# The first queries of an attention and mixer kernel: loaded by GpSimd with a cast on the way, ahead of the keys, instead of by SyncE's queue

## The chip, the cores and the metric

The kernel runs on one core of a Trainium2 chip. A core has five engines with one instruction stream each: TensorE (PE in the profile, with its weight loads shown apart as PEld), VectorE (DVE), ScalarE (ACT), GpSimd (POOL) and SyncE (SP). Transfers are issued from SyncE's, ScalarE's or GpSimd's stream. The metric is the device time of one execution in microseconds; less is better.

## The reference

Inputs are float32: q, k and v with 8 batches, 12 heads, 448 positions and head size 64, and four weight matrices. For each batch and head, scores are q times k transposed, divided by 8; the attention is the square of the positive part of the scores, divided by 448; it is multiplied with v. The heads side by side make x, of 8 x 448 x 768. A mixer follows:

```
attn = maximum(scale * (q @ k.T), 0) ** 2 / 448
x    = attn @ v, heads joined                      # 8 x 448 x 768
h    = maximum(x.T @ w_tok1, 0) @ w_tok2           # tokens: 448 -> 256 -> 448
u    = x + h.T
out  = u + maximum(u @ w_ch1, 0) @ w_ch2           # channels: 768 -> 1536 -> 768
```

## The kernel before

The 96 heads are worked in 24 groups of four heads ("slots" s; three of them make a batch). The positions of a head are 7 chunks of 64. For each group:

- Loads bring keys, queries and values to SBUF as bfloat16 (`k_raw`, `q_raw`, `v_raw`, four buffers each). The inputs are float32, so the transfer casts, and GpSimd issues it (lines 340 and 350).
- Keys and queries are transposed. For groups 0 to 8 TensorE does it (line 513), with an identity matrix `ident` that GpSimd makes, and ScalarE or VectorE copies the result from PSUM to `kqT` (lines 303 and 305). Later groups use a transposing DMA on SyncE's queue.
- Scores: 7 steps of four 64x64-weight matmuls of 448 columns (line 564, `sc_ps`). ScalarE or VectorE takes the positive part (lines 297 and 299) into `sq`, VectorE squares it in place (line 601).
- Values: 28 matmuls (line 619, `acc_ps`), then an eviction to `xT`, with the scale (lines 649 and 651).
- Token mixing: a transpose of `xT` to `x_sb` (line 704 for the first groups), the product with the first weights (line 741, `t_ps`), its positive part `r_sb`, the product with the second (line 776, `h_ps`), and on VectorE the sum u (line 788, `uT_sb`).

Per batch, channel mixing follows: line 832 (first product, 128-row weights of `wc`) and line 903 (second), whose results VectorE adds to a transposed u and SyncE stores.

The order on the engines is written out before the kernel is built. A class `Planner` holds all operations with their dependencies, an estimated duration and a rank; it steps a clock and gives every engine its next operation. GpSimd's operations alone keep the order in which they were added, that of the string `FIRST` (line 432) at the start. Where two engines can do an operation (`durs`), the planner chooses. Operations of the first batch have an earlier rank (`FRONT`). A transfer is taken to wait for a common ring, with an estimate of its `work`. So a change at the start gives a new order to all engines for the whole run.

Group 0 is special. Its first keys come in two pieces, chunks 0 and 1 (`KCUT` = 2) and chunks 2 to 6. Its queries come as float32 by SyncE's queue (line 320), into the front part of the buffer for output tiles (`out_sb`, not in use yet), and two copies, one on ScalarE and one on VectorE (`wide0`, `wide1`, line 323), cast them into `q_raw`. TensorE first runs 20 matmuls on zeros (`keep_warm`, line 427), then the transposes of all queries of group 0, 3 matmuls on zeros, the transposes of the first key piece, 3 more, the first two score steps, and the transposes of the second key piece. The query transposes wait for all of group 0's queries, the key transposes for their piece alone (line 525):

```
deps = [x for t in ts for x in (loads[s, t] if piece[1:] == (0, KC) else loads[s, t][lo > 0 :][:1])]
```

Of the kernel before, what the change touches and what calls it, by code (L numbers as in the profile page):

```python
# [49 lines left out]
class Planner:  # L50
# [6 lines left out]
    def add(self, op):  # L57
        self.ops.append(op)
        return op
# [160 lines left out]
def kernel(  # L220
# [11 lines left out]
    nc = tc.nc  # L232

    B, H, S, D = q.shape
# [4 lines left out]
    KC = 7  # L239
# [3 lines left out]
    SP = 512  # L243
# [21 lines left out]
    wt1 = sbuf.tile([128, 4, DT], BF16, name="wt1")  # L265
    wt2 = sbuf.tile([128, JC, S], BF16, name="wt2")
    wc1 = sbuf.tile([128, CC, DC], BF16, name="wc1")
    wc2 = sbuf.tile([128, EC, DM], BF16, name="wc2")
    raws = {t: [sbuf.tile([128, 2, KC * D], BF16, name=f"{t}_raw{i}") for i in range(NR)] for t in "kqv"}
# [8 lines left out]
    outs = sbuf.tile([128, NO, DM], FP32, name="out_sb")  # L278
# [5 lines left out]
    add = plan.add  # L284
# [8 lines left out]
    ANY = {"ACT": 0.424, "DVE": 0.534}  # L293
# [7 lines left out]
    def copy(o, out, ps):  # L301
        if o.on == "ACT":
            nc.scalar.activation(out, ps, AF.Copy)
        else:
            nc.vector.tensor_copy(out, ps)  # L305
# [5 lines left out]
    loads = {}  # L311

    def load(s, t):
        src = {"k": k, "q": q, "v": v}[t]
        b, i = divmod(s, GS)
        if t != "v" and s < TDMA:
            from_ = src[b, 4 * i : 4 * i + 4].rearrange("(e h) (p c) d -> (h p) e (c d)", h=2, c=KC)
            if s == 0 and t == "q":
                wide = outs.rearrange("n a m -> n (a m)")[:, : 2 * KC * D].rearrange("n (e m) -> n e m", e=2)
                o = add(Op("ldq0", "SP", lambda o: nc.sync.dma_start(out=wide, in_=from_), dur=0.5, work=1.3, late=-0.5))  # L320
                loads[s, t] = [
                    add(
                        Op(
                            f"wide{e}",
                            ("ACT", "DVE")[e],
                            lambda o, e=e: copy(o, raws[t][0][:, e], wide[:, e]),
                            [o],
                            durs=ANY,
                            slack=0.3,
                            rank=-20,  # L330
                        )
                    )
                    for e in range(2)
                ]
                return
            loads[s, t] = []
            for lo, hi in ((0, KCUT), (KCUT, KC)) if s == 0 else ((0, KC),):

                def emit(o, lo=lo, hi=hi):
                    nc.gpsimd.dma_start(  # L340
                        out=raws[t][s % NR][:, :, lo * D : hi * D], in_=from_[:, :, lo * D : hi * D]
                    )

                loads[s, t].append(add(Op(f"ld{t}{s}.{lo}", "POOL", emit, dur=0.72, work=1.41 * (hi - lo) / KC)))
            return
        for half in range(2):
            h0 = 4 * i + 2 * half

            def emit(o, half=half, h0=h0):
                ins = nc.gpsimd.dma_start(  # L350
                    out=raws[t][s % NR][64 * half : 64 * (half + 1)],
                    in_=src[b, h0 : h0 + 2].rearrange("e (p c) d -> p e (c d)", c=KC),
                )
                if o.gate is not None:
                    tc.add_manual_dep(
                        ins.ins,
                        o.gate.ins.ins.name,
                        mybir.DependencyInfo(mybir.DependencyClass.Sync, mybir.DependencyReason.DATA),
                        reason="load behind crossbar",
                    )  # L360

            o = add(Op(f"ld{t}{s}.{half}", "POOL", emit, dur=0.6, work=0.72))
            loads.setdefault((s, t), []).append(o)
# [65 lines left out]
    for x in xTs:  # L429
        nc.vector.memset(x[:, :, S:], 0.0)  # L430

    FIRST = "k0 q0 id k1 q1 v0 wt1 k2 q2 v1 v2 wt2 k3 q3 wc1 wc1 wc1 v3 k4 q4 v4 k5 q5 v5 wc2 wc2 wc2 k6 q6 v6 k7 q7 v7"
    parts = {"wc1": iter(range(3)), "wc2": iter(range(3))}
    for word in FIRST.split():
        if word == "id":
            id_op = add(Op("ident", "POOL", lambda o: make_identity(nc, ident), dur=0.6))
        elif word == "wt1":
            wt1_ops = load_wt1()
        elif word == "wt2":
            wt2_ops = load_wt2()  # L440
        elif word == "wc1":
            load_wc1(next(parts[word]), 3)
        elif word == "wc2":
            load_wc2(next(parts[word]), 3)
        else:
            load(int(word[1:]), word[0])
    for s in range(8, NS):
        for t in "kqv":
            load(s, t)
# [603 lines left out]
```

## Time and profile before

| | |
|---|---|
| median of four runs | 359.62 us (359.45 to 362.31) |
| the profiled execution | 359.45 us, of it a span of 357.7 us |
| busy PE, DVE, ACT, POOL | 351.1, 231.1, 203.1, 84.4 us |
| first channel-mixing product starts | 32.42 us |
| granted TensorE clock | 1.0 |

The span runs from the first to the last instruction. A line of a timeline has start, duration, engine, line of the kernel, operation, what it writes and reads, how many were merged, and in brackets how long the engine was idle before it and what ended that. "To landing" is the time from a transfer's issue to its semaphore. Shares of the DMA engines are of 16 engines and can pass 100%, since packets overlap.

### The profile page before, as it was taken

What the parts mean: (1) busy time and instruction counts of PE and PEld (TensorE: products, weight loads), DVE (VectorE), ACT (ScalarE), POOL (GpSimd) and SP (SyncE); (2) the same over time, 40 slices, a digit from 0 to 9 for tenths busy, and PEclk for the clock granted to TensorE, in tenths of its full rate; (3) what the DMA queues carried; (4) which work ended last, traced back from release to release, by engine and by line L of the source; (5) the groups of instructions that cost most, each with busy time, mean ns of one, the idle gap of its engine ahead of it and who ended that gap; (6) DMA issues with size and microseconds to landing.
All of it is one profiled execution on the core that took longest, in us unless ns stands there. A gap on an engine that the chain in (4) does not pass through costs nothing.

```text
span 357.7 us, 8785 instructions
## 1 busy us (share of the span) xinstructions
PE 351.1 (98%) x3506; PEld 195.2 (55%) x3506; DVE 231.1 (65%) x428; ACT 203.1 (57%) x421; POOL 84.4 (24%) x141
## 2 busy tenths in 40 slices
PE   8899999999999999999999999999999999999995
PEld 5655545554555555555555555555555555555564
DVE  4998487788697967697767877776856731111032
ACT  5998695678664767843776545752677313412400
POOL 8732522561233303330330330310000000000000
PEclk9999999999999999999999999999999999999999
DMA  8999999999998999999997999976411434113024
GB/s 133 192 212 188 173 207 174 181 219 172 200 179 142 232 183 171 153 191 167 184 116 137 154 198 202 120 124 154 105 31 22 105 81 112 29 47 88 0 66 111
DMA packets 98122, 50.62 MB, mean 142 GB/s; under 512 B 72801, under 2 KB 93857, under 8 KB 98081
## 3 DMA queue, kind: packets, MB, share of 16 engines
q1 hardware_dynamic: 74320, 28.49, 44.3%
q0 software_dynamic: 23600, 21.47, 42.3%
q8 instruction: 27, 0.44, 0.5%
q14 instruction: 15, 0.11, 0.2%
q10 hardware_dynamic: 160, 0.10, 0.1%
HBM read 43.38 MB, written 11.01 MB: 152 GB/s over the span
## 4 chain that ended last, share of the span: by engine, by line
PE 94%; DVE 3%; issue 1%; ACT 1%; ACTq 0%
PE m_ps L832 31%; PE m_ps L903 31%; PE sc_ps L564 10%; PE acc_ps L619 9%; PE t_ps L741 6%; PE h_ps L776 5%; DVE sq L601 2%; PE warm_ps L420 1%; PE kqT_ps L513 1%; PE x_ps L704 1%; DVE kqT L305 0%; ACT sq L297 0%; DVE x_sb L305 0%; DVE uT_sb L788 0%; DVE xT L651 0%
## 5 line engine op out<-in xcount | busy, mean ns | idle before, releaser
L297 ACT ACTIVATE sq<-sc_ps 128x448 bf16<-128x448 f32 x257 | 120.1, 567 | 47.4 <-PE sc_ps L564 47.4
L832 PE MATMUL m_ps<-uT_sb,wc 128*128 128x448 bf16 x576 | 116.0, 353 | 0.0
L903 PE MATMUL m_ps<-wc,r_sb 128*128 128x384 bf16 (+2 forms) x684 | 114.7, 323 | 0.0
L601 DVE TENSOR_TENSOR sq<-sq 128x896 bf16<-128x896 bf16 x168 | 97.6, 619 | 4.5 <-ACT sq L297 3.4
L297 ACT ACTIVATE r_sb<-m_ps 128x448 bf16<-128x448 f32 x96 | 52.7, 551 | 67.5 <-PE m_ps L832 67.3
L903 PEld LDWEIGHTS <-r_sb 128*128 128x128 bf16 x684 | 65.7, 98 | 44.0 <-issue 2.7
L832 PEld LDWEIGHTS <-wc 128*128 128x128 bf16 x576 | 54.9, 98 | 53.5 <-issue 5.9
L937 DVE TENSOR_TENSOR out_sb<-m_ps,u_sb 128x384 f32<-128x384 f32 (+2 forms) x57 | 31.3, 550 | 65.2 <-PE m_ps L903 65.1
L299 DVE TENSOR_SCALAR sq<-sc_ps 128x448 bf16<-128x448 f32 x79 | 47.3, 620 | 23.0 <-PE sc_ps L564 22.9
L350 POOL DMA_DIRECT2D v_raw<-in_v_dram x48 | 28.7, 605 | 128.8 <-PE sc_ps L564 111.2
L564 PE MATMUL sc_ps<-kqT 64*64 64x448 bf16 x672 | 47.5, 356 | 0.9 <-ACT sq L297 0.4
L619 PE MATMUL acc_ps<-sq,v_raw 64*64 64x448 bf16 x672 | 37.2, 350 | 0.2
L788 DVE TENSOR_TENSOR uT_sb<-h_ps,xT 128x448 bf16<-128x448 f32 x48 | 27.7, 617 | 13.7 <-PE h_ps L776 13.7
L564 PEld LDWEIGHTS <-kqT 64*64 64x64 bf16 x672 | 17.0, 105 | 22.0 <-issue 13.0
L619 PEld LDWEIGHTS <-v_raw 64*64 64x64 bf16 x672 | 19.9, 107 | 13.9 <-issue 3.1
L741 PE MATMUL t_ps<-x_sb,wt 128*128 128x256 bf16 (+1 forms) x216 | 25.1, 261 | 0.0
L776 PE MATMUL h_ps<-wt,r_sb 128*128 128x448 bf16 x96 | 22.3, 353 | 0.1
L741 PEld LDWEIGHTS <-wt 128*128 128x128 bf16 x216 | 17.9, 98 | 8.1 <-issue 5.3
L651 DVE TENSOR_SCALAR xT<-acc_ps 128x448 bf16<-128x448 f32 x24 | 14.9, 622 | 8.7 <-PE acc_ps L619 8.7
L350 POOL DMA_DIRECT2D k_raw<-in_k_dram x30 | 18.2, 620 | 6.7 <-DMA kqT<-kqi 5.1
L649 ACT ACTIVATE xT<-acc_ps 128x448 bf16<-128x448 f32 x24 | 13.3, 554 | 10.2 <-PE acc_ps L619 9.5
L350 POOL DMA_DIRECT2D q_raw<-in_q_dram x30 | 18.4, 637 | 1.7 <-issue 1.6
(38 smaller groups left out, 119.0 us busy)
## 6 DMA issues: line engine op xcount, KB each, us to landing
out_dram<-out_sb SPq DMA_DIRECT2D x54, 192.0 KB, 2.9
v_raw<-in_v_dram POOLq DMA_DIRECT2D x48, 112.0 KB, 5.6
wc<-in_moe_w_ch_dram POOLq DMA_DIRECT2D x6, 768.0 KB, 14.1
k_raw<-in_k_dram POOLq DMA_DIRECT2D x30, 112.0 KB, 5.7
q_raw<-in_q_dram POOLq DMA_DIRECT2D x30, 112.0 KB, 6.3
k_raw<-in_k_dram POOLq DMA_DIRECT2D x8, 224.0 KB, 9.1
q_raw<-in_q_dram POOLq DMA_DIRECT2D x8, 224.0 KB, 8.6
u_sb<-uT_sb SPq DMA_TRANSPOSE x48, 4.9
```

Of the source, the lines that this page charges most:

```text
L297: nc.scalar.activation(out, ps, AF.Relu)
L299: nc.vector.tensor_scalar(out=out, in0=ps, scalar1=0.0, scalar2=None, op0=ALU.max)
L350: ins = nc.gpsimd.dma_start(out=raws[t][s % NR][64 * half : 64 * (half + 1)], in_=src[b, h0 : h0 + 2].rearrange("e (p c) d -> p e (c d)", ...
L564: nc.tensor.matmul(o.ps[z][64 * y : 64 * (y + 1), :S], lhsT=kT[rows, half, c, :], rhs=qT[rows, half, :, :], start=True, stop=True, skip_gr ...
L601: lambda o: nc.vector.tensor_tensor(out=buf, in0=buf, in1=buf, op=ALU.mult),
L619: nc.tensor.matmul(o.ps[half][64 * e : 64 * (e + 1), :S], lhsT=r[rows, e, c * D : (c + 1) * D], rhs=sq[rows, e, :], start=(c == 0), stop=( ...
L741: nc.tensor.matmul(o.ps[:, j, lo * 128 : hi * 128], lhsT=wt1[:, c, j * 128 : (j + 1) * 128], rhs=x_sb[:, lo:hi, c, :], start=(c == 0), sto ...
L776: nc.tensor.matmul(o.ps[:, :S], lhsT=r1[:, j, a * 128 : (a + 1) * 128], rhs=wt2[:, j, :], start=(j == 0), stop=(j == JC - 1),)
L788: nc.vector.tensor_tensor(out=uTs[bb % 2][:, 2 * i + a, off : off + S].rearrange("n (c p) -> n c p", c=KC), in0=t2.ps[:, :S].rearrange("n ...
L832: nc.tensor.matmul(o.ps[:, :S], lhsT=wc1[:, g, e * 128 : (e + 1) * 128], rhs=uT[:, g, off : off + S], start=(g == 0), stop=(g == CC - 1), ...
L903: nc.tensor.matmul(o.ps[:, :m], lhsT=r2[:, e, t * 128 : (t + 1) * 128], rhs=wc2[:, e, cols], start=(e == 0), stop=(e == EC - 1), skip_grou ...
L937: nc.vector.tensor_tensor(out=out_sb[:, cols].rearrange("n (g d) -> n g d", d=128), in0=u.ps[:, :m].rearrange("n (g d) -> n g d", d=128), ...
```

## The change

The special case of group 0's queries goes: no load by SyncE, no float32 copy in `out_sb`, no casts by ScalarE and VectorE. The queries take the branch that the first keys take, where GpSimd issues the load with the cast on the way. Since that branch cuts group 0 at `KCUT`, the queries come in two transfers, chunks 0 and 1 and chunks 2 to 6. In `FIRST` they are put ahead of the keys.

```
@@ load(s, t)
-            if s == 0 and t == "q":
-                wide = outs.rearrange("n a m -> n (a m)")[:, : 2 * KC * D].rearrange("n (e m) -> n e m", e=2)
-                o = add(Op("ldq0", "SP", lambda o: nc.sync.dma_start(out=wide, in_=from_), dur=0.5, work=1.3, late=-0.5))
-                loads[s, t] = [
-                    add(
-                        Op(
-                            f"wide{e}",
-                            ("ACT", "DVE")[e],
-                            lambda o, e=e: copy(o, raws[t][0][:, e], wide[:, e]),
-                            [o],
-                            durs=ANY,
-                            slack=0.3,
-                            rank=-20,
-                        )
-                    )
-                    for e in range(2)
-                ]
-                return
             loads[s, t] = []
             for lo, hi in ((0, KCUT), (KCUT, KC)) if s == 0 else ((0, KC),):
...
-    FIRST = "k0 q0 id k1 q1 v0 wt1 k2 q2 v1 v2 wt2 k3 q3 wc1 wc1 wc1 v3 ...
+    FIRST = "q0 k0 id k1 q1 v0 wt1 k2 q2 v1 v2 wt2 k3 q3 wc1 wc1 wc1 v3 ...
```

More of the change, by code (lines that the diff above doesn't have):

```diff
@@ L430 @@
         nc.vector.memset(x[:, :, S:], 0.0)
-    FIRST = "k0 q0 id k1 q1 v0 wt1 k2 q2 v1 v2 wt2 k3 q3 wc1 wc1 wc1 v3 k4 q4 v4 k5 q5 v5 wc2 wc2 wc2 k6 q6 v6 k7 q7 v7"
+    FIRST = "q0 k0 id k1 q1 v0 wt1 k2 q2 v1 v2 wt2 k3 q3 wc1 wc1 wc1 v3 k4 q4 v4 k5 q5 v5 wc2 wc2 wc2 k6 q6 v6 k7 q7 v7"
     parts = {"wc1": iter(range(3)), "wc2": iter(range(3))}
```

## The prediction

> **What bounds the kernel now.** I read first the page's busy shares and chain, then each engine's busy time by stage, then the first ten microseconds instruction by instruction, and last the DMA records of those microseconds.
>
> The page and its chain of work that ended last:
> ```profile
> PE 351.1 (98%) x3506; PEld 195.2 (55%) x3506; DVE 231.1 (65%) x428; ACT 203.1 (57%) x421; POOL 84.4 (24%) x141
> PE 94%; DVE 3%; issue 1%; ACT 1%; ACTq 0%
> ```
> TensorE carries 94% of the chain. Where the rest lies shows in the busy times by stage (columns: stretch, its length, then busy time and instruction count of PE, PEld, DVE, ACT, POOL; clock, DMA share, GB/s):
> ```profile
> 0.00:10.00 10.00, 8.41 (x131) 5.34 (x135) 4.65 (x14) 5.93 (x12) 8.17 (x17) 1.00 0.85 134
> 10.00:20.00 10.00, 9.00 (x232) 6.09 (x224) 10.00 (x20) 10.00 (x25) 7.30 (x11) 1.00 1.27 201
> 20.00:32.60 12.60, 12.26 (x203) 6.84 (x198) 11.92 (x25) 12.57 (x30) 3.37 (x5) 1.00 1.12 204
> 32.60:60.00 27.40, 27.40 (x368) 14.52 (x366) 18.98 (x34) 21.23 (x43) 9.43 (x14) 1.00 1.27 184
> ```
> From 10 to 32.6 us VectorE and ScalarE are full (10.00 of 10, 11.92 and 12.57 of 12.6): this front is theirs. At 32.6 us the first channel-mixing product starts, and from there TensorE is full (27.40 of 27.40; nothing is listed under TensorE's waits from there to 345 us). So the run is a front of 32.6 us, a dense TensorE part and a short tail. What delays the first channel product delays the end by as much, unless the dense part becomes shorter.
>
> The change touches the first 7 us. Their timeline (start, duration, engine, line, operation):
> ```profile
> 0.74 0.46 SPq L320 DMA_DIRECT2D out_sb<-in_q_dram  x1
> 1.25 1.58 POOL L340 DMA_DIRECT2D k_raw<-in_k_dram  x2 [0.81 <-POOLq L1037]
> 2.81 0.24 POOL masks.py:197 MEMSET ident<- 128x128 bf16 x1
> 3.36 0.72 POOL L340 DMA_DIRECT2D k_raw<-in_k_dram  x1
> ...
> 4.17 0.58 ACT L303 ACTIVATE q_raw<-out_sb 128x448 bf16<-128x448 f32 x1 [2.15 <-DMA out_sb<-in_q_dram]
> ...
> 4.93 0.41 PE L513 MATMUL kqT_ps<-ident,q_raw 64*64 64x64 bf16 x28
> ...
> 5.71 0.26 PE L513 MATMUL kqT_ps<-ident,k_raw 64*64 64x64 bf16 x8
> ...
> 6.33 0.57 PE L564 MATMUL sc_ps<-kqT 64*64 64x448 bf16 x8
> 6.54 0.40 PEld L513 LDWEIGHTS <-k_raw 64*64 64x64 bf16 x20
> ```
> The query load is issued at 0.74 and lands 3.4 us later, at 4.14; two casts at 4.17 make the operand, and TensorE starts the query transposes at 4.93. The keys' two pieces, issued at 1.25 and 2.04, land 3.5 and 4.0 us after their issue, at 4.75 and 6.05, in time for their transposes at 5.71 and 6.54. Those times to landing are from the list of DMA issues:
> ```profile
> out_sb<-in_q_dram SPq DMA_DIRECT2D x1, 448.0 KB, 3.4
> k_raw<-in_k_dram POOLq DMA_DIRECT2D x1, 160.0 KB, 4.0
> k_raw<-in_k_dram POOLq DMA_DIRECT2D x1, 64.0 KB, 3.5
> ```
> The queues' shares, half a microsecond at a time, show the plain query transfer alone on the DMA engines up to 3.0 us (100 of its packets and 102.8% between 2.5 and 3.0), while GpSimd's queue moves its first packet only after 3.0 and the keys' 512 data packets until about 5.5.
>
> **What the Trainium skill says.** "DMA: Bandwidth & Descriptors", section "SWDGE vs HWDGE vs iDMA": a cast during the transfer can only be issued from GpSimd, and "HWDGE is dedicated RTL that emits descriptors without software in the loop". The trace agrees in kind: first packet about 1.1 us after SyncE's issue, about 1.9 us after GpSimd's. The same page, "Issuing engines are not separate DMA queues": all issuers end on the same 16 engines. The trace agrees: the two queues share the engines from 3.0 to 3.8 us. "TensorE: Matmul & The Clock Gate", "What's actually happening": the clock falls back after an idle window of some 3.4 us. The gap that I find below is 0.9 us, so I take no loss of clock; no run here shows it.
>
> **The change part by part.**
>
> *Removed.* One issue on SyncE (0.46 us) and two casts (0.58 and 0.39 us, side by side, 4.17 to 4.75, and 0.2 until TensorE starts). SyncE has nothing else to do until the first transposes of u, and ScalarE and VectorE were idle before the casts (2.15 and 2.41 us), so the instructions themselves are worth nothing. What goes from the path is the casts' step of 4.93 − 4.14 = 0.8 us.
>
> *Added.* The words say one issue; in the order as built there are two, because the query now takes the split of the first keys: 128x2x128 and 128x2x320. Each costs GpSimd 0.72 to 0.84 us (duration of such an issue), 1.55 together.
>
> *Moved back on GpSimd.* Behind them stand the two key pieces, the identity matrix (0.53 us), then keys and queries of the second group, values, token weights and all later loads. The issues slip by 1.55 us: keys at 2.8 and 3.6, identity done at 5.2, second group at 4.9.
>
> *Landing.* The query pieces stand where the keys stood: landed by 4.75 and 6.05; without the plain transfer beside them from 3.0 to 3.8 some 0.2 us sooner, so 5.9. The identity (5.2) is earlier. The query transposes, which need both pieces, start at about 5.9 instead of 4.93: +0.9 to 1.0. The keys queue behind: the two pieces took GpSimd's queue from 3.1 to 5.5, 2.4 us; less the sharing about 2.1. The first key piece is then served from 5.3 to 6.1 and lands near 6.5, the second near 7.9. The first key transposes run at 6.7 (5.71 before, +1.0), the others at 7.9 (6.54, +1.35). Keys and queries of the second group wait for the same queue, which is done with the first group at 3.1 + 2 × 2.1 = 7.3 instead of 5.5, less about 0.35 in which the DMA engines were not full between 5.0 and 6.0 us (84.8 and 68.0% where the half microsecond before has 118.6): +1.4. The values and weights behind were not what anything waited for. Bounds for this start: +0.8 (the query's landing alone is late, the rest catches up) to +2.1 (the whole service is added). I take **+1.4**.
>
> Can VectorE and ScalarE take it back? Not in the order given: they are full to 32.6 us. VectorE's idle time between 8.1 and 32.6 us is 0.7 us.
>
> *The order after.* The planner writes a new order for all five queues. Counting instructions from the built order: the last transposed copy that the front needs (x_sb of the third group, done at 30.43 us) has before it on VectorE, after the first group's third copy to kqT (done at 7.79), 21 squares and 4 relus now and 23 and 6 in the changed kernel; the other 17 are equal in number. Four more at 0.535 us (four squares from 23.66 to 25.82) are 2.1 us. That stretch lasts 22.64 us and its instructions sum to 36 × 0.535 + 6 × 0.335 = 21.3, so 1.4 us of it is idle time; if all of that filled, 0.8 us of the 2.1 would remain. Between 0.8 and 2.1 I take **+1.0**, nearer the low end because relus go to VectorE where the planner sees it waiting. Two matmuls of token mixing (0.38 us) come after the first channel product instead of before it: **+0.4**. TensorE changes 116 times instead of 120 between quarter-array and full-array work, at some 0.11 us each (eight token-mixing matmuls take 0.98 us, at the channel rate of 1.95 us for twelve of 384 columns they would take 0.87), and has one filler less (0.09): **−0.5**. Matmul counts are otherwise equal, and so is the tail.
>
> *Sum.* 1.4 + 1.0 + 0.4 − 0.5 = +2.3 us. The profiled run took 359.45 us (span 357.7 and 1.75 around it): 361.75. The median of the four runs is 0.17 higher than the profiled run: 361.9.
>
> **The rivals.**
> - *The start alone* (chance 0.20): the changed order on VectorE only fills gaps, and +1.4 + 0.4 − 0.5, or a little less, remains: 360.8. For it: the planner gives priority to the front. Against: the idle time is only 1.4 us.
> - *A stall in the dense part* (0.24): a new order is right only as far as the planner's landing times are. Now not one TensorE wait is listed after 32.6 us. TensorE is in order, so one matmul whose score eviction or transposing DMA is late holds all behind it. Loads wait up to 4.4 us for channel weights; half of that once, on top of 2.3, gives 364.1. It decides as soon as one wait of about 1.3 us appears. It ends slower by over 1%.
> - *No loss* (0.08), on the other side: if scores of the first group, already waiting on evictions, hide the later keys and the new order packs tighter, only −0.5 from fewer array changes remains, and +0.2 of delay: 359.3.
> - *The change isn't what it says*: that holds for "one issue"; the second issue is in the sum above and is no separate case.
>
> **How the numbers follow.** Forecast, 361.9, chance 0.48, own range 361.0 to 363.3. 1% is 3.6 us, about what a measurement of this kernel can tell from no change; above 363.2 lie most of the stall (0.2) and an edge of the forecast (0.04): slower 0.24. Faster by 1% would need a gain that no step offers: 0.02. Same: 0.74. The 8-in-10 range leaves out the no-loss case and the upper part of the stall: 360.0 to 364.6.
>
> **What would show it.** The query transposes at 5.9 and the first scores at 7.2 us; kqT's third copy near 9.1; the first channel product near 35 us; TensorE full after it. It is wrong if the first channel product comes before 34 us with the end late all the same (then the dense part lost), or if waits of TensorE appear after it, or if TensorE's first scores run at half the rate because the idle gap cost it its clock.

## The result, and the profile after

The changed kernel takes 1.008 times as long as the kernel before, 95% interval 1.0057 to 1.0103: about 2.9 us more (0.008 × 359.6), which on the 359.6 us that the forecast started from makes some 362.5 us. The plain medians, 364.14 us of 35 runs and 360.21 of 56, lie further apart; they are of all executions, and the ratio leaves the disturbed ones out. The forecast was 361.9 in a range of 360.0 to 364.6 and "within 1%", and both hold. The profiled execution took 361.88 us, 2.4 more than that of the kernel before; forecast for it was +2.3. It is the fourth shortest of the changed kernel's runs, so its trace shows the change at its best. From line 317 on, lines of the changed kernel have numbers that are 18 lower: 513 became 495, 564 became 546, 832 became 814.

The page of the changed kernel, its busy shares and the chain by engine:
```profile
PE 352.2 (98%) x3505; PEld 195.8 (54%) x3505; DVE 232.3 (65%) x430; ACT 201.0 (56%) x417; POOL 85.8 (24%) x143
PE 91%; ACT 3%; DVE 2%; DMA 1%; issue 1%; POOL 1%; ACTq 0%; POOLq 0%
```
Transfers and GpSimd have come into the chain. Its busy time by stage, in the same columns as before:
```profile
0.00:10.00 10.00, 7.99 (x107) 4.97 (x108) 2.87 (x10) 3.98 (x8) 8.88 (x18) 1.00 0.74 87
10.00:20.00 10.00, 8.72 (x212) 5.51 (x213) 9.97 (x20) 10.00 (x25) 6.96 (x12) 1.00 1.24 188
20.00:32.60 12.60, 11.85 (x208) 6.34 (x204) 12.60 (x26) 11.83 (x28) 3.70 (x6) 1.00 1.09 193
32.60:60.00 27.40, 27.24 (x356) 14.91 (x356) 20.16 (x38) 20.94 (x46) 9.55 (x14) 1.00 1.24 183
```
In the first 10 us VectorE and ScalarE do 2.87 and 3.98 us of work instead of 4.65 and 5.93; the casts explain only 1.0 of these 3.7 us; the rest is work that starts later. From 20 to 32.6 VectorE is completely full (12.60, was 11.92). The start in its timeline:
```profile
1.25 1.58 POOL L322 DMA_DIRECT2D q_raw<-in_q_dram  x2 [0.80 <-POOLq L1019]
2.80 1.46 POOL L322 DMA_DIRECT2D k_raw<-in_k_dram  x2
4.56 0.29 POOL masks.py:199 TENSOR_SCALAR_AFFINE_SELECT ident<-ident 128x128 bf16<-128x128 bf16 x1
...
5.75 0.35 PE L495 MATMUL kqT_ps<-ident,q_raw 64*64 64x64 bf16 x20 [0.23 <-DMA q_raw<-in_q_dram]
...
6.47 0.26 PE L495 MATMUL kqT_ps<-ident,k_raw 64*64 64x64 bf16 x8
...
8.28 0.35 PE L495 MATMUL kqT_ps<-ident,k_raw 64*64 64x64 bf16 x20 [0.61 <-DMA k_raw<-in_k_dram]
...
8.71 0.33 DVE L305 COPY kqT<-kqT_ps 128x320 bf16<-128x320 bf16 x1 [0.39 <-PE kqT_ps L495]
```
TensorE now waits for the second query piece until 5.75 and for the second key piece until 8.28; the key transposes ran at 6.73 before. The third copy to kqT, which closes the start, ends at 9.04 instead of 7.79: +1.25. Further down, the end of the front in the changed kernel:
```profile
32.40 0.76 DVE L305 COPY x_sb<-x_ps 128x512 bf16<-128x512 bf16 x2
34.49 0.92 PE L814 MATMUL m_ps<-uT_sb,wc 128*128 128x448 bf16 x4
39.50 1.52 PE L601 MATMUL acc_ps<-sq,v_raw 64*64 64x448 bf16 x28
```
The same marks in the kernel before, with the third copy to kqT:
```profile
7.48 0.31 DVE L305 COPY kqT<-kqT_ps 128x320 bf16<-128x320 bf16 x1
...
29.68 0.75 DVE L305 COPY x_sb<-x_ps 128x512 bf16<-128x512 bf16 x2
32.42 4.70 PE L832 MATMUL m_ps<-uT_sb,wc 128*128 128x448 bf16 x24
37.05 1.52 PE L619 MATMUL acc_ps<-sq,v_raw 64*64 64x448 bf16 x28
```
x_sb of the third group ends at 33.16 (30.43 before), and the 28 value matmuls after the first four channel tiles start at 39.50 (37.05 before). Ahead of this value product both kernels have done the same work but for a filler, which makes it a good mark: +2.45 there, +2.4 at the end of the span.

### The profile page after: what moved, and what is told of

It reads as the page before. It is cut to its first block, busy times and chain, and to the rows that moved or that the text cites. A ratio compares the mean times of both kernels' runs of the same rounds, so it can differ in the third digit from the quotient of the medians.

```text
span 360.1 us, 8776 instructions
## 1 busy us (share of the span) xinstructions
PE 352.2 (98%) x3505; PEld 195.8 (54%) x3505; DVE 232.3 (65%) x430; ACT 201.0 (56%) x417; POOL 85.8 (24%) x143
## 4 chain that ended last, share of the span: by engine, by line
PE 91%; ACT 3%; DVE 2%; DMA 1%; issue 1%; POOL 1%; ACTq 0%; POOLq 0%
PE m_ps L885 31%; PE m_ps L814 31%; PE sc_ps L546 9%; PE acc_ps L601 8%; PE t_ps L723 6%; PE h_ps L758 5%; ACT sq L297 3%; DMA k_raw<-in_k_dram 1%; PE kqT_ps L495 1%; DVE sq L583 1%; PE x_ps L686 1%; POOL q_raw L322 0%; DVE uT_sb L770 0%; DVE sq L299 0%; DVE x_sb L305 0%
## 5 line engine op out<-in xcount | busy, mean ns | idle before, releaser
L299 DVE TENSOR_SCALAR sq<-sc_ps 128x448 bf16<-128x448 f32 x81 | 48.5, 620 | 20.5 <-PE sc_ps L546 20.4
L546 PE MATMUL sc_ps<-kqT 64*64 64x448 bf16 x672 | 49.1, 357 | 1.6 <-DVE kqT L305 0.5
L546 PEld LDWEIGHTS <-kqT 64*64 64x64 bf16 x672 | 17.5, 105 | 25.1 <-issue 16.4
L297 ACT ACTIVATE r_sb<-t_ps 128x512 bf16<-128x512 f32 (+1 forms) x27 | 15.8, 604 | 12.9 <-PE t_ps L723 12.8
```

Of the source, the lines that this page charges most:

```text
L297: nc.scalar.activation(out, ps, AF.Relu)
L299: nc.vector.tensor_scalar(out=out, in0=ps, scalar1=0.0, scalar2=None, op0=ALU.max)
L546: nc.tensor.matmul(o.ps[z][64 * y : 64 * (y + 1), :S], lhsT=kT[rows, half, c, :], rhs=qT[rows, half, :, :], start=True, stop=True, skip_gr ...
```

## The experiments

The planner knows of a transfer only through its estimate, so order and transfers can be changed one at a time. Each trace gives three numbers: when the third copy to kqT ends (the start), how long from there to the value product of the third group (the front), and how long from there to the end of the span (the dense part, with the waits of TensorE that are listed after 60 us).

| kernel | transfers | order | start | front | dense part | waits in it |
|---|---|---|---|---|---|---|
| before | SyncE | old | 7.79 | 29.26 | 320.65 | 0 |
| changed | two pieces | new | 9.04 | 30.46 | 320.60 | 0 |
| e1_old_order | two pieces | old | 9.00 | 29.45 | 323.35 | 2.6 |
| e1b_one_issue_old_order | one piece | old | 8.10 | 29.46 | 320.64 | 0 |
| e2_new_order | SyncE | new | 8.53 | 31.87 | 321.70 | 1.0 |
| e3_one_issue | one piece | its own | 8.45 | 29.77 | 320.48 | 0 |
| e4_two_halves | two halves | old | 8.75 | 29.19 | 320.66 | 0 |
| e5_one_issue_gap | one piece, gap | old | 8.57 | 29.26 | 320.67 | 0 |
| e6_new_order_again | SyncE | new | 7.97 | 30.22 | 321.81 | 1.2 |
| e7_four_more | SyncE | old, four more | 8.81 | 31.07 | 320.62 | 0 |
| e8_warm17 | SyncE | old | 7.62 | 29.21 | 320.57 | 0 |
| e9_after_warm17 | two pieces | new | 9.71 | 30.25 | 323.64 | 1.9 |
| e10_after_again | two pieces | new | 8.86 | 30.53 | 322.11 | 1.1 |
| e11_after_third | two pieces | new | 8.90 | 30.81 | 326.39 | 3.2 |

**The transfers alone** (e1_old_order). The planner still sees SyncE's load and two casts, but GpSimd's two issues are written out in the place of the load, and nothing in the place of the casts:
```
-o = add(Op("ldq0", "SP", lambda o: nc.sync.dma_start(out=wide, in_=from_), dur=0.5, ...
+def early(pieces):
+    for lo, hi in pieces:
+        nc.gpsimd.dma_start(out=raws[t][0][:, :, lo * D : hi * D], in_=from_[:, :, lo * D : hi * D])
+o = add(Op("ldq0", "SP", lambda o: early(((0, KCUT), (KCUT, KC))), dur=0.5, ...
-            lambda o, e=e: copy(o, raws[t][0][:, e], wide[:, e]),
+            lambda o: None,
```


> The changed kernel's transfers (queries in two GpSimd issues ahead of the keys, no casts) in the order of the kernel before on every engine. Theory (the start and the order each cost about half): the third copy to kqT ends near 9.0 us (7.79 before, 9.04 in the changed kernel), the value product of the third group near 37.05 + 1.3 = 38.3, the run +1.3 us, ratio about 1.0035. Rival 'all is the start': the same start, but the value product near 39.5 and the run +2.4 us, ratio 1.007. Rival 'all is the order': ratio 1.000.

Ratio 1.0048 (1.0019 to 1.0078). The third copy ends at 9.00 and the value product starts at 38.45, as the first theory has it; "all is the start" (39.5) and "all is the order" (37.1) both fail. The trace has one gap of 2.6 us on TensorE, put down to issue, that no other trace shows (its run, 363.62 us, is 2 us above the median); the start and the front lie ahead of it.

**The order alone** (e2_new_order, and the same kernel again as e6_new_order_again). The planner sees the changed kernel's operations, but what is written out is the old load and the casts:
```
 def emit(o, lo=lo, hi=hi):
+    if s == 0 and t == "q":
+        if lo == 0:
+            wide = outs.rearrange("n a m -> n (a m)")[:, : 2 * KC * D].rearrange("n (e m) -> n e m", e=2)
+            nc.sync.dma_start(out=wide, in_=from_)
+            nc.scalar.activation(raws[t][0][:, 0], wide[:, 0], AF.Copy)
+            nc.vector.tensor_copy(raws[t][0][:, 1], wide[:, 1])
+        return
     nc.gpsimd.dma_start(
```


> The kernel before's transfers (queries by SyncE, two casts) in the order of the changed kernel on every engine. Theory: the third copy to kqT ends at 7.8 us as before, the value product of the third group near 37.05 + 1.2 = 38.3, the run +1.1 us, ratio about 1.003. Rival 'all is the start': value product at 37.1, ratio 1.000. Rival 'all is the order': value product at 39.5, ratio 1.007.

> The kernel before's transfers in the changed kernel's order once more, for a trace at full clock. Theory (the order alone costs 1.0 to 1.5 us by what it puts ahead on VectorE): third copy to kqT ends at 7.8 us, value product of the third group at 38.1 to 38.6, the end later by the same. Rival (the order costs the 2.6 us that the timing showed, by something after the front): value product at 38.1 to 38.6 and the end later than that by 1 us or more.

Ratios 1.0073 (1.0046 to 1.0100) and 1.0050 (1.0020 to 1.0080): more than the 1.003 expected. The first trace can't be read for the front. Its busy time by stretch has the clock as the third number from the end:
```profile
11.00:13.00 2.00, 1.11 (x43) 0.50 (x32) 2.00 (x5) 2.00 (x6) 1.98 (x4) 0.99 1.28 194
13.00:14.00 1.00, 1.00 (x16) 0.88 (x12) 1.00 (x3) 1.00 (x4) 1.00 (x2) 0.50 1.27 202
14.00:15.00 1.00, 1.00 (x17) 0.77 (x12) 1.00 (x3) 1.00 (x4) 0.77 (x2) 0.50 1.26 195
15.00:16.00 1.00, 1.00 (x16) 0.67 (x10) 0.92 (x2) 0.35 (x1) 0.54 (x1) 0.50 1.26 200
16.00:17.00 1.00, 1.00 (x16) 0.52 (x13) 0.00 (x0) 0.49 (x2) 1.00 (x3) 0.81 1.27 203
```
TensorE ran at half clock from 13 to about 16.4 us. The second trace is at full clock. Its front is 30.22 us, 0.96 longer than that of the kernel before; with the two-piece transfers the new order costs 30.46 − 29.45 = 1.01. So the order costs about 1.0 us in the front with either kind of transfer. Besides, both traces have a wait of TensorE in the dense part. The waits of TensorE in e6_new_order_again after 60 us, and its timeline there (rows of other engines left out):
```profile
PE sc_ps L553 <- DVE sq L299: 1.2, 1, 1.2
```
```profile
182.42 0.36 PE L553 MATMUL sc_ps<-kqT 64*64 64x448 bf16 x4
...
182.76 0.62 DVE L305 COPY kqi<-q_raw 128x896 bf16<-128x896 bf16 x1 [1.11 <-DMA q_raw<-in_q_dram]
...
183.30 0.61 DVE L299 TENSOR_SCALAR sq<-sc_ps 128x448 bf16<-128x448 f32 x1
183.97 0.38 PE L553 MATMUL sc_ps<-kqT 64*64 64x448 bf16 x4 [1.19 <-DVE sq L299]
```
On VectorE a copy of queries that have not landed (1.11 us) stands ahead of the score eviction that TensorE needs a bank from. The copy of the same group's keys, at 181.03, had already waited 2.46 us. The profile names no cause for that, but the second half of these keys landed then: it was issued near 172.3 and took 8.7 us. So both the theory and its rival hold: 1.0 in the front, 1.2 after it.

**One issue** (e1b_one_issue_old_order, and e3_one_issue with the planner's own order): `early(((0, KC),))` in the first kernel above; in the changed kernel
```
-for lo, hi in ((0, KCUT), (KCUT, KC)) if s == 0 else ((0, KC),):
+for lo, hi in ((0, KCUT), (KCUT, KC)) if s == 0 and t == "k" else ((0, KC),):
```


> As the first, but the queries in one GpSimd issue, in the order of the kernel before. Theory (issue slots and packets both delay the keys): GpSimd slips by 0.75 instead of 1.55 us, half as many query packets, so the third copy to kqT ends near 8.4 us and the run is +0.6 us, ratio 1.0015. Rival (bytes alone count): third copy near 9.0, +1.3 us as with two issues.

> The change in one issue, with the order that the planner makes of it. Theory: +0.6 us from the start as with one issue in the old order, and what the new order adds, between -0.5 and +1.5: ratio 1.000 to 1.006. Rival 'all is the start': +0.6 us only.

Ratios 1.0007 (0.9986 to 1.0028) and 1.0007 (0.9972 to 1.0041). With one issue the change costs nothing that these runs can measure: third copies at 8.10 and 8.45 us. Its own order (e3_one_issue) has 21 squares and 5 relus in the stretch that was counted in the prediction, one instruction more than the old one, and a front of 29.77. That is 0.3 us longer than with the same transfer in the old order and 0.5 longer than in the kernel before; one such instruction is 0.54 us.

**Issues or packets** (e4_two_halves, e5_one_issue_gap). Two issues cut by head pair, `raws[t][0][:, e]` from `from_[:, e]`, keep the rows whole; the other kernel has one issue and a memset of 128x448 on GpSimd behind it.

> Order of the kernel before; the queries in two GpSimd issues, but cut by head pair and not by chunk, so that each row stays whole: 256 data packets as with one issue, not 512. Theory 'packets' (the short packets of the second cut delay the keys): the value product of the third group near 37.6 us, as with one issue (37.56), ratio 1.001. Rival 'issues' (GpSimd's time for one more issue delays the keys): near 38.4, as with two issues (38.45), ratio 1.004.

> Order of the kernel before; the queries in one GpSimd issue, then a memset that holds GpSimd for about the time of one issue before the keys. Theory 'packets': value product near 37.6 us, ratio 1.001. Rival 'issues': near 38.3, ratio 1.004.

Ratios 1.0028 (0.9994 to 1.0062) and 1.0009 (0.9973 to 1.0046). The value product starts at 37.94 and 37.83, between the theories, so these marks alone decide nothing: in both traces the 20 matmuls on zeros took the full 4.45 us, and the query transposes had to wait for them until 5.44. The landings tell more. The lists of DMA issues of the first microseconds have the second key piece, first in e1_old_order, then in e4_two_halves:
```profile
k_raw<-in_k_dram POOLq DMA_DIRECT2D x1, 160.0 KB, 4.7
```
```profile
k_raw<-in_k_dram POOLq DMA_DIRECT2D x1, 160.0 KB, 3.7
```
It is issued near 3.5 us in the first and 3.2 in the second (the halves cost GpSimd 1.23 us together, the chunk pieces 1.57), and lands at 8.2 and 6.9. TensorE waits 0.54 us for it in the first and not in the second. One issue less and a gap instead (e5_one_issue_gap: 3.2 + 4.0 = 7.2) also ends without that wait. The landing varies from trace to trace: with whole rows it lies at 6.9, 7.2, 7.3 and 7.7 (the last two with one issue and no gap), with the cut through the rows at 7.7 in e9_after_warm17 and at 8.1 to 8.2 in the four others, on average 0.8 later. With whole rows an issue at 3.2 instead of 2.8 did not make it later. So the cut through the rows makes the keys late; that GpSimd's time has a part in it is not seen.

**Four instructions more on VectorE** (e7_four_more), in the kernel before:
```
 nc.vector.memset(wt1, 0.0)
+nc.vector.memset(more, 0.0)
...
 else:
+    if s == 2:
+        for _ in range(4):
+            nc.vector.tensor_tensor(out=more, in0=more, in1=more, op=ALU.mult)
     nc.vector.tensor_scalar(
```
`more` is a part of the output buffer that is not in use yet.

> The kernel before, with four more squares of 128x896 on VectorE, of a buffer that nothing reads, ahead of the third group's eviction to xT: as many instructions as the changed kernel's order has more in this stretch. Theory (VectorE's count sets the front): 4 x 0.535 less the 0.5 us that it waits there now: x_sb of the third group ends 1.6 us later (30.43 to 32.0), the value product of that group near 38.5, ratio 1.004. Rival (the front has slack, the order costs elsewhere): value product within 0.4 us of 37.05, ratio 1.000.

Ratio 1.0062 (1.0041 to 1.0084). The front is 31.07 us, 1.81 longer, against 1.6 expected; the wait is seen where it arises, in the waits of TensorE:
```profile
PE x_ps L709 <- DVE xT L656: 1.5, 1, 1.5
```
So the number of instructions on VectorE ahead of this point sets the front, and what lengthens the front lengthens the run.

**Fewer matmuls on zeros** (e8_warm17 in the kernel before, e9_after_warm17 in the changed one): `WARM = 17, 3, 3`.

> The kernel before with 17 instead of 20 matmuls on zeros at the start (WARM), the order else unchanged. Theory (in the kernel before the query transposes start when the matmuls on zeros end, at 5.0 to 5.5 us by how long the clock stays low, and not when the queries land): the query transposes start at 4.9 us, third copy to kqT at 7.8, the run 0.3 to 0.5 us shorter on average, ratio 0.999. Rival (the landing of the queries sets the start): no change, ratio 1.000. Rival (fewer matmuls leave the clock low for longer): slower by 0.5 us or more.

> The changed kernel with 17 matmuls on zeros. Theory (here the landings set the start): the second part of the query transposes still waits for its DMA until 5.7 to 5.8 us, the third copy to kqT still ends near 9.0, ratio against the kernel before 1.007 to 1.009 as with 20. Rival (the matmuls on zeros set it here too): third copy 0.3 us or more earlier.

Ratios 1.0019 (0.9982 to 1.0055) and 1.0111 (1.0026 to 1.0195, four runs). The first trace fits the theory of what sets the start:
```profile
1.06 3.33 PE L420 MATMUL warm_ps<-warm 128*128 128x256 bf16 x17 [1.06 <-DVE warm L415]
4.76 0.41 PE L513 MATMUL kqT_ps<-ident,q_raw 64*64 64x64 bf16 x28 [0.38 <-ACT q_raw L303]
```
The 17 matmuls were done, and TensorE waited 0.38 us for ScalarE's cast. The third copy ends at 7.62, earlier than in any other trace. Yet the kernel isn't shown to be shorter: the interval contains a loss and a small gain, and the traced run, 359.25 us, was the shortest of the 14. In e9_after_warm17 the rival that the clock stays low for longer is seen at work. Its timeline:
```profile
6.11 0.82 PE L402 MATMUL warm_ps<-warm 128*128 128x256 bf16 x3
7.11 0.82 PE L402 MATMUL warm_ps<-warm 128*128 128x256 bf16 x3
9.03 0.73 PE L402 MATMUL warm_ps<-warm 128*128 128x256 bf16 x3
```
Three matmuls on zeros last 0.50 us in the other traces, but for the first three in some of them (0.57 to 0.82), and here the first two groups last 0.82 and the third 0.73. From this it is inferred that the clock stayed low until about 9 us; the column of the granted clock has 1.00 there. The third copy ends at 9.71 instead of 9.04. So in the changed kernel neither theory's number came out. One trace doesn't show that the 17 matmuls did this: with the same 17 in e8_warm17 such groups took 0.50.

**The changed kernel twice more** (e10_after_again, e11_after_third), without an edit.

> The changed kernel once more, for a second trace. Theory (the new order also brings a TensorE wait of 1 to 2 us into the dense part in some executions, as in three of the four traces of that order so far): the value product of the third group starts 30.3 to 30.6 us after the third copy to kqT ends, and in one of this and the next trace a wait of TensorE of 1 us or more appears after 60 us. Rival (those waits belong to the edits of those kernels): no wait above 0.5 us after 60 us in either.

> As the run before it, for a third trace of the changed kernel: same expectation for the two together.

Single runs of 363.30 and 367.87 us, the second at a mean clock of 0.995. The fronts are 30.53 and 30.81 us, the second a little outside the expectation, with a wait of 0.63 us for the second group's queries in it. Both traces have the dense part's wait. In the second its largest is
```profile
187.01 0.62 DVE L305 COPY kqi<-q_raw 128x896 bf16<-128x896 bf16 x1 [2.39 <-DMA q_raw<-in_q_dram]
187.55 0.61 DVE L299 TENSOR_SCALAR sq<-sc_ps 128x448 bf16<-128x448 f32 x1
188.22 0.38 PE L546 MATMUL sc_ps<-kqT 64*64 64x448 bf16 x4 [2.42 <-DVE sq L299]
```
the same pair of instructions as in e6_new_order_again. In e2_new_order and e10_after_again TensorE waits for the same eviction (0.97 and 1.09 us, at 186.06 and 185.36); in both, as in e6_new_order_again and e11_after_third, the copy of the keys ahead had waited 2.4 to 3.4 us. In e9_after_warm17 the wait is another one, for an addition to the output on VectorE at 126.86. With the old order or the planner's own for one issue, seven of eight traces have no such wait, and the eighth has the gap of another kind. Late queries alone don't make one: in e7_four_more the copy waited 1.82 us for them, and no wait of TensorE followed.

## Why the prediction was right, step by step

*The bound.* Right: every delay that reached the value product of the third group came out at the end. Without the listed waits the dense part is 320.5 to 320.8 us in all traces but three (321.0 in e10_after_again, 321.7 in e9_after_warm17, 323.2 in e11_after_third, whose clock halved from 189 to 192.4 us, right after the wait of 2.42).

*The casts' step of 0.8 us.* This failed. The query transposes of the kernel before didn't start when the casts were done but when the 20 matmuls on zeros ended. In the profile shown the two fell together, at about 5.0; with the same transfers the transposes started at 5.10, 5.44 and 5.44 in three other traces, and with 17 matmuls at 4.76. The error did no harm to the sum, which rested on the new landing.

*The landings.* Forecast: query transposes 5.9, first key transposes 6.7, the others 7.9, third copy "near 9.1". Measured: 5.75 for the last of the queries (the first eight ran at 5.26, since each matmul waits only for its own piece), 6.47, 8.28 and 9.04. The queries and keys of the second group were forecast 1.4 late; their query transposes ran at 11.73 instead of 10.40, +1.33. Most of this was estimated from the time of the packets in GpSimd's queue, and the packets of the cut rows are the cause that e4_two_halves and e5_one_issue_gap show.

*The size of the start, +1.4.* The profiles give +1.25. But the profile of the kernel before began early. Its transfers, with 20 matmuls on zeros, give third copies at 7.79, 7.97, 8.53 and 8.81 (mean 8.28); two pieces give 8.86, 8.90, 9.00 and 9.04 (mean 8.95). So the start costs some 0.7 us on average, and the 1.25 of this pair of traces was half its luck.

*The order, +1.0, and token mixing, +0.4.* Between the two profiles the front of the table, which holds both terms, is 1.20 us longer, and 0.96 and 1.01 in the two pairs of traces in which only the order differs. e7_four_more shows that instructions on VectorE do this. The terms one by one came out otherwise and partly cancelled. From the third copy to the end of x_sb the new order costs 1.48 us (24.12 instead of 22.64), so less of VectorE's idle time was filled than the forecast took. The first channel product then follows after 1.33 us instead of 1.99, a gain that the sum did not have: two matmuls of token mixing now come behind it, and eight score matmuls ahead of the end of x_sb. From the first channel product (+2.07) to the value product (+2.45) the moved matmuls give 0.38 back. The −0.5 for fewer array changes isn't seen: the dense part is 0.05 us shorter.

*The rival of a stall in the dense part* (chance 0.24, +2.2 us) did not show in the first profile, but five of the six traces with the new order have waits of 1.0 to 3.2 us there. "One matmul whose score eviction ... is late holds all behind it" is what four of them show, with VectorE as the place where it is held. The runs are thus a mixture of the forecast and this rival. Their spread fits that: of the runs with a mean clock of 0.998 or more, the 23 of the changed kernel lie between 361.39 and 366.12 us, and 14 of the 15 of e3_one_issue between 360.01 and 360.94. An estimate from the traces with 20 matmuls: 0.7 for the start, 1.0 for the order, 0.8 for the waits (mean of 0, 1.0, 1.2 and 1.1), together 2.5, against 2.9 from the ratio, whose interval is 2.1 to 3.7. With the 3.2 of e11_after_third, whose clock was lower, the waits make 1.3 and the sum 3.0. So the forecast of +2.3 came near with one term too large and one left to a rival: the range held for the reasons that it gave. That the single number lies so close to the first profile is in part luck.

*The clock.* "I take no loss of clock" is right for the profile shown. It was too simple: e2_new_order and e11_after_third show half clock for 3.4 us, and e9_after_warm17 slow matmuls for the first 9.

*Still open:* why loads of the later groups land late in the new plan. Where the score eviction is late, the second half of the keys ahead of it landed 8.6 to 9.2 us after its issue (three traces; for e10_after_again the landing isn't known), and 5.3, 6.0 and 6.2 after it in the kernel before, the changed kernel's first trace and e7_four_more. Nothing that the change touches moves at that time except the order of the engines, and what slows these loads was not tried. No version tried here is shown to beat the kernel before; the one with a single issue can't be told from it.

## What to carry to other kernels

Where a planner writes the order of the engines, a change of one transfer is two changes: separate them by giving the planner the old operations and writing out the new ones, and the reverse. In a stretch where one engine is full, count the instructions that a new order puts on it ahead of the next stage's first operation. A start that ends on warm-up matmuls has no exact time: look at several traces before a gain or loss of under 1 us is read off one pair.

## What was not expected of the hardware

- The same 20 matmuls on zeros took 3.65 to 4.45 us from execution to execution, and later work with them.
- The clock of TensorE halved for 3.4 us, from 13 to 16.4 us, in e2_new_order, after two microseconds with TensorE 1.11 of 2.00 busy and no listed wait above 0.73. The page of the Trainium skill that the prediction used, "TensorE: Matmul & The Clock Gate" ("What's actually happening"), speaks of an idle window of about 3.4 us. Here the stretch ahead was thinly used, not idle. That alone doesn't explain it: in e1_old_order TensorE was busy for 1.05 of the same two microseconds, and its clock stayed at 1.00. In e11_after_third the clock halved for 3.4 us too, after a wait of 2.42. What sets off such a dip is open; the same section's 3.4 us for a window agrees with its length.
- A load of the same 224 KB and the same number of issues, cut so that rows stay whole, let the next transfer land 1.3 us earlier (6.9 instead of 8.2) than one cut through the rows. Over all traces with the queries on GpSimd the difference is 0.8 us.
